# A fused attention, mixture-of-experts and MLP kernel: three kinds of instruction change places in the front end

## The chip, the cores and the metric

The kernel runs on one core of one Trainium2 chip. A core has five engines with queues of their own: TensorE (PE in the profile; its weight loads are PEld), VectorE (DVE), ScalarE (ACT), GpSimd (POOL) and SyncE (SP), which here issues most of the DMAs. Each engine takes its instructions in the order in which the program put them, so an instruction that waits holds up all that stand behind it on that engine. The metric is the device time of one execution in microseconds; lower is better.

## The reference

Three stages follow one another; the result of each is the input of the next. Only the last one's result is returned.

```python
def _attn_ref(q, k, v, phi):          # (4, 8, 576, 64), 32 memory slots
    a = np.exp(phi - np.max(phi, axis=2, keepdims=True))
    a = a / (np.sum(a, axis=2, keepdims=True) + 1e-09)
    k_m = np.einsum('bhsm,bhsd->bhmd', a, k)
    v_m = np.einsum('bhsm,bhsd->bhmd', a, v)
    scores = np.matmul(q, k_m.transpose(0, 1, 3, 2)) / np.sqrt(64)
    attn = softmax(scores)
    return np.matmul(attn, v_m)
def _moe_ref(x, w_gate, w_noise, noise, w1, w2):   # 2304 tokens, 512 wide, 8 experts of 1024
    noisy = x @ w_gate + np.log1p(np.exp(x @ w_noise)) * noise
    top2, top2_w = the two largest of noisy, softmax over these two
    for e in range(8):
        for k in range(2):
            mask = top2[:, k] == e
            out[mask] += top2_w[mask, k, None] * (np.maximum(x[mask] @ w1[e], 0.0) @ w2[e])
def _moe2_ref(x, w_in, w_out):        # 512 -> 2048 -> 512
    h = x @ w_in
    return (h * np.cos(h)) @ w_out
```

## The kernel before

**Stages.** The 2304 tokens are 18 tiles of 128, t0 to t17. The *front end* is the attention with the routing: four batches' memory keys and values (`k_gen(b)`), then the 18 tiles (`t_gen(t)`), then two routings, of tiles 0 to 7 (`route(0)`) and of tiles 8 to 17 (`route(1)`). The *experts* follow: each has a first product (`l1`, eight column groups f, 24 matmuls each for expert 0's first part) and a second (`l2`), run on tokens that POOL gathers by index (`xg`) and SP transposes (`x`). The MLP (`m1`, `m2_`) is last. Expert weights come as float32 (`raw`) and are split into a high and a low float16 half (`w`): four squares per weight for the scale (`junk`, line 176), four copies for the high halves (`w_hi`, line 201, on ACT), four subtractions for the low ones (`w_lo`, line 204, on DVE). The squares and splits of expert 0's weights lie between the attention's tiles on ACT.

**One batch, `k_gen`.** DVE takes the maximum of phi (`mx`, line 556), ACT the exponential (`ew`, 563), PE transposes it (`et`), ACT copies it out (`e`), PE makes keys and values (`kp`, 40 matmuls), DVE and ACT scale them (`kd`, 590; `vm`, 593), PE transposes the keys (`pk`), and DVE and ACT each copy a half of them into `bdk` (601, 602), which all tiles of the batch need. `bdv` holds the values.

**One tile, `t_gen`.** PE makes the scores (`sc`, 655), DVE subtracts their maxima (`smx`, 660; `sd`, 663), ACT takes the exponential, DVE the sum and its reciprocal (`ssm`, 668 and 669), POOL multiplies (`d`), PE transposes (`pt`), ACT copies (`e2T`, 677), PE makes the output (`x`, 685). ACT then reads `x` twice: the scaled rows (`xs`, 690) and the routing logits (`lgb`, line 696, shown as `rlgb` or `rt`). ACT makes the high float16 half (`hl`, 700), POOL the low one (701), and SP stores both. `x` has one buffer: the next tile's output waits until the logits are copied. The scores' buffers are halves of one tile, and so are those of `pt`.

**What sets the order.** Every step has a planned time (`at`, `stages`); `issue` writes the steps out by these times, and a scheduler then orders each engine's instructions by priority and by its own idea of when their inputs are there. `gated(key)` puts an instruction behind another, named one (`last[key]`), in that order; `chain` does so for a whole series. For expert 0's weights a table names what each square and split stands behind:

```python
(w_square, 0): ("t7A", "t8A", "t9A", "t10A"),
(w_hi, 0): ("t12A", "t13A", "t14A", "t15A"),
```

Here `t12A` is set by tile 12's copy `xs`. PE's `l1` for f = 2 stands behind the second routing's `rank` matmuls (`gated("rank")`, line 850), and these stand behind both f = 0 and f = 1 in PE's order.

Of the kernel before, what the change touches and what calls it, by code (L numbers as in the profile page):

```python
# [60 lines left out]
def fused_kernel(ctx, tc, phiT, qT, kv, wgn, noise, w1, w2, wi, wo, out):  # L61
# [154 lines left out]
    def chain(key, fn, *a, **kw):  # L216

        with gated(key):
            last[key] = fn(*a, **kw)  # L219
# [122 lines left out]
    def route(g):  # L342
# [25 lines left out]
        for k in range(2):  # L368
# [10 lines left out]
            if k == 0:  # L379
                V.scalar_tensor_tensor(y, oh[0][:, ts, :], -3.0e38, y, op0=OP.mult, op1=OP.add)  # L380
                yield
        V.tensor_tensor(m16[:, ts, :], oh[0][:, ts, :], oh[1][:, ts, :], op=OP.add)
        d = rg(g, "d", n)
# [164 lines left out]
    for k in range(2):  # L548
        bdk.append(ap.tile([P, 4, 2 * M], F32, tag=f"bdk{k}", name="bdk", bufs=1))
        G.memset(bdk[k], 0.0)  # L550

    def k_gen(b):

        ph = ph_t.pop(b)
        mx = ap.tile([P, 2], F32, tag="mx", name="mx", bufs=1)
        V.tensor_reduce(mx, ph, axis=AX.X, op=OP.max)
        V.tensor_scalar(mx, mx, -1.0, None, op0=OP.mult)
# [4 lines left out]
        for g in range(2):  # L562
            A.activation(ew[:, g, o:o + S], ph[:, g, :], AF.Exp, bias=mx[:, g:g + 1], accum_out=den[:, g:g + 1])
        V.tensor_scalar(den, den, eps, None, op0=OP.add)
# [24 lines left out]
        for g in range(2):  # L589
            V.tensor_scalar(kd[:, g], kp[:, g, None, 0:D].to_broadcast([P, 2, D]), den[:, g:g + 1], None, op0=OP.mult)  # L590
        vm = ap.tile([P, 2, D], F32, tag="vm", name="vm", bufs=1)
# [9 lines left out]
        last[f"bdk{b}V"] = V.tensor_copy(bk[0:64, :, 0:M], pv[0:64, :, 0, :])  # L601
        A.activation(bk[64:128, :, M:], pv[64:128, :, 1, :], AF.Copy)
        yield
# [45 lines left out]
    def t_gen(t):  # L649
# [39 lines left out]
        with gated(f"t{ahead}E"):  # L689
            last[f"t{t}A"] = A.activation(xs.rearrange("p (g d) -> p g d", g=2), x[:, :, 0:256], AF.Copy,  # L690
                                          scale=sT[:, 0, t:t + 1])
        g = ROUTE_OF[t]
        if t == GROUPS[g][0]:
            n = GROUPS[g][1] - GROUPS[g][0]
            lgb[g] = rg(g, "lgb", n, 2, 2 * E)
        A.activation(lgb[g][:, t - GROUPS[g][0]], x[:, :, 256:272], AF.Copy)
        yield
# [54 lines left out]
    for b in range(B):  # L752
        stages(k_gen(b), [k_start[b] + x for x in k_steps])
    for i in range(NT):
# [100 lines left out]
    def l1_out(e, part, f):  # L855
        n = (parts[part][1] - parts[part][0]) * P
        hi, lo = hT[e, part]
        ph = prod.pop((e, part, f))
        chain("A", A.activation, hi[:, f, :], ph[:, :n], AF.Relu)
        chain("V", V.scalar_tensor_tensor, lo[:, f, :], ph[:, :n], 0.0, hi[:, f, :], op0=OP.max, op1=OP.subtract)  # L860

# [406 lines left out]
```

## Time and profile before

| | us |
|---|---|
| three timed runs | 933.47, 937.98, 939.71 |
| their median | 937.98 |
| span of the profiled execution | 936.9 |
| PE busy in it | 883.3 (94%) |
| DVE, ACT, POOL busy | 581.2, 468.1, 213.1 |

The span runs from the first instruction to the last; the page gives no other time for the profiled execution, and it lies 1.1 us below the median and inside the spread of the three runs (6.2 us, 0.7%). PE is busy nearly all the time from the experts on, and not in the first seventh of the span. Busy shares of PE say little in themselves, since the ends of matmuls are modelled; the granted clock stands beside them.

### The profile page before, as it was taken

The page shows a single profiled execution, that of the slowest core. Times are in us where ns is not written, and L with a number is a line of the kernel's source. Part 1 is how long each engine was busy: PE and PEld are TensorE (multiplying, and loading weights), DVE is VectorE, ACT ScalarE, POOL GpSimd, SP SyncE. Part 2 cuts the span into 40 slices and gives each one's busy share as a digit, 9 for nine tenths or more (in the row PEclk, how much of TensorE's full clock was granted, in tenths as well). Part 3 has the DMA queues.
Part 4 walks back from the last instruction along what each step waited for, and adds up shares of the span by engine and source line. Part 5 has one row for each costly group of instructions (what it writes and reads, how often), then busy time and mean ns, then how long its engine had stood idle before and what let it go on. Part 6 is the DMA issues. An engine that isn't in the chain of part 4 may idle for free. (4 is left out here: it accounts for less than half of the span.)

```text
span 936.9 us, 14173 instructions
## 1 busy us (share of the span) xinstructions
PE 883.3 (94%) x5368; PEld 512.9 (55%) x5368; DVE 581.2 (62%) x1266; ACT 468.1 (50%) x830; POOL 213.1 (23%) x234
## 2 busy tenths in 40 slices
PE   4897489999999999999999999999999999999997
PEld 3676265655647475655646565564444444444564
DVE  2557572476757575776762457787875774555564
ACT  3487624666766676667772333444432432322242
POOL 1255312120010101010000124334432522221221
PEclk9897589999999999999999999999999999999999
DMA  9971239888797769799653454222401510200010
GB/s 350 396 270 68 91 83 268 268 220 296 243 303 240 206 242 292 250 263 336 206 185 136 114 202 90 69 68 57 102 1 12 130 40 1 78 12 1 1 45 23
DMA packets 108246, 146.55 MB, mean 156 GB/s; under 512 B 65808, under 2 KB 66448, under 8 KB 106128
## 3 DMA queue, kind: packets, MB, share of 16 engines
q1 hardware_dynamic: 89536, 103.56, 35.9%
q0 software_dynamic: 6080, 19.93, 7.4%
q10 hardware_dynamic: 12560, 22.13, 6.7%
q8 instruction: 43, 0.70, 0.3%
q14 instruction: 27, 0.22, 0.1%
HBM read 95.26 MB, written 35.13 MB: 139 GB/s over the span
## 5 line engine op out<-in xcount | busy, mean ns | idle before, releaser
L219 PE MATMUL h<-x,w 128*128 128x384 f16 (+1 forms) x1536 | 215.3, 301 | 9.7 <-DMA x<-xg 9.3
L219 PE MATMUL y<-w,hT 128*128 128x512 f16 x960 | 210.7, 379 | 2.2 <-issue 2.2
L219 PE MATMUL g<-x2T,win 128*128 128x256 f16 (+1 forms) x1152 | 202.5, 326 | 5.8 <-DVE ty L1043 4.4
L219 PE MATMUL o<-wout,gT 128*128 128x512 f16 x864 | 202.1, 379 | 0.2
L219 PEld LDWEIGHTS <-w 128*128 128x128 f16 x1536 | 151.5, 99 | 68.7 <-DMA x<-xg 8.8
L219 PEld LDWEIGHTS <-win 128*128 128x128 f16 x1152 | 112.6, 98 | 90.2 <-issue 8.0
L219 PEld LDWEIGHTS <-hT 128*128 128x128 f16 x960 | 93.8, 99 | 111.4 <-issue 2.7
L1045 POOL TENSOR_TENSOR gT<-ty,gT 128x256 f16<-128x256 f32 (+1 forms) x96 | 92.7, 967 | 252.8 <-ACT gT L1044 252.7
L1042 ACT ACTIVATE tt<-tt,hp 128x256 f32<-128x256 f32 (+1 forms) x96 | 58.9, 614 | 164.3 <-DVE tt L1041 150.1
L219 PEld LDWEIGHTS <-gT 128*128 128x128 f16 x864 | 84.1, 98 | 93.4 <-POOL gT L1045 2.1
L219 DVE SCALAR_TENSOR_TENSOR w<-raw,wsc,w 128x1024 f16<-128x1024 f32 x64 | 81.1, 1288 | 32.6 <-ACT w L219 32.6
L219 DVE SCALAR_TENSOR_TENSOR hT<-h,hT 128x384 f16<-128x384 f32 (+1 forms) x128 | 61.4, 487 | 63.2 <-ACT hT L219 62.9
L1039 DVE SCALAR_TENSOR_TENSOR ty<-g,wis,bct 128x256 f32<-128x256 f32 (+1 forms) x96 | 58.8, 612 | 65.1 <-PE g L219 65.1
L219 ACT ACTIVATE hT<-h 128x384 f16<-128x384 f32 (+1 forms) x128 | 55.3, 435 | 73.4 <-PE h L219 70.5
L1043 DVE SCALAR_TENSOR_TENSOR ty<-g,fac,tt 128x256 f32<-128x256 f32 (+1 forms) x96 | 59.1, 616 | 52.8 <-ACT tt L1042 52.2
L1044 ACT ACTIVATE gT<-ty 128x256 f16<-128x256 f32 (+1 forms) x96 | 50.2, 523 | 64.5 <-DVE ty L1043 64.4
L219 ACT ACTIVATE w<-raw,wsc 128x1024 f16<-128x1024 f32 x64 | 71.6, 1139 | 4.4 <-ACT o L219 2.1
L825 POOL DMA_INDIRECT xg<-xd,idxB x24 | 24.1, 1006 | 218.3 <-DMA x<-xg 207.7
L1041 DVE SCALAR_TENSOR_TENSOR tt<-tt,ty 128x256 f32<-128x256 f32 (+1 forms) x96 | 68.9, 718 | 2.6
L219 ACT ACTIVATE junk<-raw 128x1024 bf16<-128x1024 f32 x64 | 67.3, 1051 | 3.9 <-ACT o L219 3.4
L219 ACT ACTIVATE o<-y,ysc 128x512 f32<-128x512 f32 x40 | 27.4, 686 | 70.6 <-PE y L219 70.4
L963 POOL DMA_INDIRECT y<-yd,sidx x36 | 36.3, 1010 | 88.4 <-DMA yd<-o 80.7
(234 smaller groups left out, 714.1 us busy)
## 6 DMA issues: line engine op xcount, KB each, us to landing
raw<-in_w SPq DMA_DIRECT2D x32, 1024.0 KB, 9.1
yd<-o ACTq DMA_DIRECT2D x40, 256.0 KB, 5.0
kvt<-in_kv SPq DMA_DIRECT2D x9, 1024.0 KB, 15.6
cvt<-in_wi SPq DMA_DIRECT2D x8, 1024.0 KB, 6.5
wst<-cvt SPq DMA_DIRECT2D x16, 512.0 KB, 3.4
cvt<-in_wo SPq DMA_DIRECT2D x8, 1024.0 KB, 9.1
yd<-zero ACTq DMA_DIRECT2D x13, 512.0 KB, 5.5
xd<-hl SPq DMA_DIRECT2D x18, 256.0 KB, 2.1
```

The costliest lines, as they stand in the source:

```text
L219: last[key] = fn(*a, **kw)
L825: G.indirect_dma_start(out=g, out_offset=None, in_=xd[0:NA * P] if part == 0 else xd, in_offset=bass.IndirectOffsetOnAxis(ap=idx[:, col:co ...
L963: G.indirect_dma_start(out=y, out_offset=None, in_=yd[0:rows], in_offset=bass.IndirectOffsetOnAxis(ap=sidx[:, t, k:k + 1], axis=0))
L1039: V.scalar_tensor_tensor(y, ph[:, :n], wis[:, 2 * E + c:2 * E + c + 1], bct[j], op0=OP.mult, op1=OP.mult)
L1041: V.scalar_tensor_tensor(t, t, MAGIC, y, op0=OP.subtract, op1=OP.subtract)
L1042: A.activation(t, t, AF.Sin, bias=hp, scale=-2.0 * math.pi)
L1043: V.scalar_tensor_tensor(y, ph[:, :n], fac[:, c:c + 1], t, op0=OP.mult, op1=OP.mult)
L1044: A.activation(g[:, 0, :n], y, AF.Copy)
L1045: G.tensor_tensor(g[:, 1, :n], y, g[:, 0, :n], op=OP.subtract)
```

## The change

Five edits, all in the order of the front end; no instruction's work changes.

1. `last["t{t}A"]` is set by the copy of the logits in place of the copy `xs`. What the table puts behind a tile (a square or a split of expert 0's weights) now stands behind the logits.
2. The maxima of phi of batches 1, 2 and 3 are put behind other work on DVE: behind batch 0's scaled keys, behind tile 0's reciprocal, behind tile 3's.
3. Batch 1's exponentials are put behind ACT's half of batch 0's `bdk`, and batch 1's first step is planned at 16.9 in place of 15.0.
4. The first low half of `hT` (expert 0, part 0, f = 0) is put behind the second routing's mask sum `m16`.
5. Two keys are set for this (`kd0`, `bdk0A`, `m16` with the routing's number).

```diff
-        V.tensor_tensor(m16[:, ts, :], oh[0][:, ts, :], oh[1][:, ts, :], op=OP.add)
+        last[f"m16{g}"] = V.tensor_tensor(m16[:, ts, :], oh[0][:, ts, :], oh[1][:, ts, :], op=OP.add)
...
+    MX_AFTER = {1: "kd0", 2: "t0V", 3: "t3V"}
...
-        V.tensor_reduce(mx, ph, axis=AX.X, op=OP.max)
+        with gated(MX_AFTER.get(b)):
+            V.tensor_reduce(mx, ph, axis=AX.X, op=OP.max)
...
-            A.activation(ew[:, g, o:o + S], ph[:, g, :], AF.Exp, bias=mx[:, g:g + 1], accum_out=den[:, g:g + 1])
+            with gated("bdk0A" if b == 1 else None):
+                A.activation(ew[:, g, o:o + S], ph[:, g, :], AF.Exp, bias=mx[:, g:g + 1], accum_out=den[:, g:g + 1])
...
-            last[f"t{t}A"] = A.activation(xs.rearrange("p (g d) -> p g d", g=2), x[:, :, 0:256], AF.Copy,
+            A.activation(xs.rearrange("p (g d) -> p g d", g=2), x[:, :, 0:256], AF.Copy,
                                           scale=sT[:, 0, t:t + 1])
...
-        A.activation(lgb[g][:, t - GROUPS[g][0]], x[:, :, 256:272], AF.Copy)
+        last[f"t{t}A"] = A.activation(lgb[g][:, t - GROUPS[g][0]], x[:, :, 256:272], AF.Copy)
...
-        stages(k_gen(b), [k_start[b] + x for x in k_steps])
+        stages(k_gen(b), [16.9 if b == 1 and x == -8.0 else k_start[b] + x for x in k_steps])
...
-        chain("V", V.scalar_tensor_tensor, lo[:, f, :], ph[:, :n], 0.0, hi[:, f, :], op0=OP.max, op1=OP.subtract)
+        with gated("m161") if (e, part, f) == (0, 0, 0) else nullcontext():
+            chain("V", V.scalar_tensor_tensor, lo[:, f, :], ph[:, :n], 0.0, hi[:, f, :], op0=OP.max, op1=OP.subtract)
```

Line numbers of the changed kernel are 3 to 5 higher from the edits on (690 becomes 694, 655 becomes 659).

**ACT at tile 13**, before and then changed: `xs_1131` is tile 13's copy, `rt_887` the logits of the second routing, `w_1101` the high half of expert 0's first weight.

```order
L690 ACTIVATE xs_1131<-x_1117,sT_108 128x512
L219 ACTIVATE w_1101<-raw_634,wsc_113 128x1024
L696 ACTIVATE rt_887<-x_1117 128x32
L677 ACTIVATE e2T_1144<-pt_155 128x256
L700 ACTIVATE hl_1135<-xs_1131 128x512
```

```order
L694 ACTIVATE xs_1131<-x_1117,sT_108 128x512
L700 ACTIVATE rt_887<-x_1117 128x32
L219 ACTIVATE w_1101<-raw_634,wsc_113 128x1024
L681 ACTIVATE e2T_1144<-pt_155 128x256
L704 ACTIVATE hl_1135<-xs_1131 128x512
```

The split and the logits have changed places; it is so at tiles 12 to 15 with the splits and at tiles 7 to 10 with the squares.

**PE at tiles 11 to 13**, before and then changed: `x_1035`, `x_1069` and `x_1117` are the outputs of tiles 11, 12 and 13, the two `sc` rows the scores of tiles 16 and 17, `sums` belongs to the weights' scale.

```order
L655 MATMUL sc_154<-bdk_141,qt_632 128x64 x4
L685 MATMUL x_1035<-bdv_712,e2T_955 128x272 x2
L219 MATMUL sums_1022<-wmx_109,ones32_111 128x5
L675 MATMUL pt_155<-ident_73,d_1045 128x128 x2
L655 MATMUL sc_154<-bdk_141,qt_632 128x64 x4
L685 MATMUL x_1069<-bdv_712,e2T_1032 128x272 x2
L675 MATMUL pt_155<-ident_73,d_1079 128x128 x2
```

```order
L689 MATMUL x_1035<-bdv_712,e2T_955 128x272 x2
L659 MATMUL sc_154<-bdk_141,qt_632 128x64 x4
L219 MATMUL sums_1022<-wmx_109,ones32_111 128x5
L679 MATMUL pt_155<-ident_73,d_1045 128x128 x2
L689 MATMUL x_1069<-bdv_712,e2T_1032 128x272 x2
L679 MATMUL pt_155<-ident_73,d_1079 128x128 x2
L659 MATMUL sc_154<-bdk_141,qt_632 128x64 x4
```

The outputs of tiles 11 and 12 now stand ahead of the scores of tiles 16 and 17.

**DVE from the end of batch 0 on**, before and then changed: `mx_263` and `mx_274` are batch 1's maximum, `mx_422` batch 2's, `kd_273` and `kd_263` batch 0's keys, `smx_337` and `smx_391` the maxima of tiles 0 and 1, `ssm_386` tile 0's sum.

```order
L556 TENSOR_REDUCE mx_263<-ph_161 128x2
L557 TENSOR_SCALAR mx_263<-mx_263 128x2
L590 TENSOR_SCALAR kd_273<-kp_222,den_198 128x128 x2
L601 COPY bdk_139<-pk_279 64x4x32
L564 TENSOR_SCALAR den_268<-den_268 128x2
L565 RECIPROCAL den_268<-den_268 128x2
L660 TENSOR_REDUCE smx_337<-sc_154 128x8
L560 MEMSET ew_425 128x2x64
L663 TENSOR_TENSOR sd0_143<-sc_154,smx_337 128x8x32
L668 TENSOR_REDUCE ssm_386<-sd0_143 128x8
L556 TENSOR_REDUCE mx_422<-ph_161 128x2
L669 RECIPROCAL ssm_386<-ssm_386 128x8
```

```order
L594 TENSOR_SCALAR kd_263<-kp_222,den_198 128x128 x2
L559 TENSOR_REDUCE mx_274<-ph_161 128x2
L605 COPY bdk_139<-pk_269 64x4x32
L560 TENSOR_SCALAR mx_274<-mx_274 128x2
L568 TENSOR_SCALAR den_279<-den_279 128x2
L569 RECIPROCAL den_279<-den_279 128x2
L664 TENSOR_REDUCE smx_337<-sc_154 128x8
L667 TENSOR_TENSOR sd0_143<-sc_154,smx_337 128x8x32
L672 TENSOR_REDUCE ssm_386<-sd0_143 128x8
L673 RECIPROCAL ssm_386<-ssm_386 128x8
L559 TENSOR_REDUCE mx_422<-ph_161 128x2
L664 TENSOR_REDUCE smx_391<-sc_154 128x8
```

Batch 1's maximum has moved behind batch 0's keys, and batch 2's behind the whole of tile 0's row work; batch 3's, further on, from ahead of tile 2's `smx` to behind tile 3's reciprocal.

## Rows read from the trace of the kernel before

**Rows 1.** Stretches of the span: length, engines' busy time, granted clock, DMA share.

```profile
core 0 of [0], span 936.9 us
core 0: us, PE busy (x) PEld busy (x) DVE busy (x) ACT busy (x) POOL busy (x), PEclk, DMA share, GB/s
40.00:50.00 10.00, 10.00 (x102) 7.33 (x102) 4.28 (x15) 5.39 (x15) 4.38 (x5) 0.86 1.04 389
80.00:90.00 10.00, 8.47 (x32) 5.89 (x32) 7.91 (x35) 4.88 (x13) 3.69 (x5) 0.52 0.14 53
160.00:200.00 40.00, 40.00 (x257) 24.96 (x256) 25.21 (x59) 26.62 (x44) 7.27 (x8) 1.00 0.83 251
```

**Rows 2.** Timeline, tiles 12 to 17: start, us, engine, line, operation [idle before, releaser].

```profile
85.93 0.69 ACT L690 ACTIVATE xs<-x,sT 128x512 f32<-128x512 f32 x1 [2.39 <-PE x L685]
86.52 1.14 ACT L219 ACTIVATE w<-raw,wsc 128x1024 f16<-128x1024 f32 x1
...
87.55 0.19 ACT L696 ACTIVATE rt<-x 128x32 f32<-128x32 f32 x1
87.63 0.38 ACT L677 ACTIVATE e2T<-pt 128x256 f32<-128x256 f32 x1
...
87.79 2.09 PE L685 MATMUL x<-bdv,e2T 128*64 128x272 f32 x8 [1.53 <-ACT rt L696]
...
88.20 0.64 ACT L700 ACTIVATE hl<-xs 128x512 f16<-128x512 f32 x1
...
90.00 0.69 ACT L690 ACTIVATE xs<-x,sT 128x512 f32<-128x512 f32 x1 [1.06 <-PE x L685]
...
102.42 0.69 ACT L690 ACTIVATE xs<-x,sT 128x512 f32<-128x512 f32 x1 [1.54 <-PE x L685]
...
103.24 2.18 PE L685 MATMUL x<-bdv,e2T 128*128 128x272 f32 x4 [0.93 <-ACT rt L696]
...
105.52 0.69 ACT L690 ACTIVATE xs<-x,sT 128x512 f32<-128x512 f32 x1 [0.78 <-PE tab L433]
```

**Rows 3.** Timeline, tiles 10 and 11 with the scores of tile 16.

```profile
76.45 0.69 ACT L690 ACTIVATE xs<-x,sT 128x512 f32<-128x512 f32 x1
...
78.98 1.10 PE L655 MATMUL sc<-bdk,qt 128*128 128x64 f32 x8 [1.17 <-DVE sbt L629]
...
79.92 1.64 PE L685 MATMUL x<-bdv,e2T 128*128 128x272 f32 x4
...
81.66 0.69 ACT L690 ACTIVATE xs<-x,sT 128x512 f32<-128x512 f32 x1 [2.16 <-PE x L685]
```

**Rows 4.** Timeline, maxima of phi of batches 1 to 3 and their neighbours.

```profile
14.90 1.35 DVE L556 TENSOR_REDUCE mx<-ph 128x2 f32<-128x1152 f32 x1 [4.01 <-DMA ph<-in_phiT]
...
16.36 0.60 DVE L590 TENSOR_SCALAR kd<-kp,den 128x128 f32<-128x128 f32 x2
...
25.79 1.35 DVE L556 TENSOR_REDUCE mx<-ph 128x2 f32<-128x1152 f32 x1 [1.03 <-DMA ph<-in_phiT]
...
28.05 0.61 DVE L590 TENSOR_SCALAR kd<-kp,den 128x128 f32<-128x128 f32 x2
...
35.16 1.35 DVE L556 TENSOR_REDUCE mx<-ph 128x2 f32<-128x1152 f32 x1 [2.64 <-DMA ph<-in_phiT]
36.43 0.41 DVE L660 TENSOR_REDUCE smx<-sc 128x8 f32<-128x256 f32 x1
...
37.35 1.10 PE L655 MATMUL sc<-bdk,qt 128*128 128x64 f32 x8 [2.59 <-DVE sd L663]
```

**Rows 5.** Timeline, from the last tile to the experts.

```profile
107.98 1.16 POOL L701 TENSOR_TENSOR hl<-xs,hl 128x512 f16<-128x512 f32 x1 [1.95 <-issue]
...
119.44 5.30 PE L219 MATMUL h<-x,w 128*128 128x256 f16 x24 [8.71 <-DMA x<-xg]
...
122.63 0.42 DVE L219 SCALAR_TENSOR_TENSOR hT<-h,hT 128x256 f16<-128x256 f32 x1 [3.89 <-ACT hT L219]
...
124.53 0.33 PE L390 MATMUL rank<-m,after 128*128 128x80 f16 x1
...
145.32 11.86 PE L219 MATMUL h<-x,w 128*128 128x384 f16 x72 [0.60 <-DMA x<-xg]
```

More of the change, by code (lines that the diff above doesn't have):

```diff
@@ L589, in k_gen @@
         for g in range(2):
-            V.tensor_scalar(kd[:, g], kp[:, g, None, 0:D].to_broadcast([P, 2, D]), den[:, g:g + 1], None, op0=OP.mult)
+            last[f"kd{b}"] = V.tensor_scalar(kd[:, g], kp[:, g, None, 0:D].to_broadcast([P, 2, D]), den[:, g:g + 1], None, op0=OP.mult)
         vm = ap.tile([P, 2, D], F32, tag="vm", name="vm", bufs=1)
@@ L601, in k_gen @@
         last[f"bdk{b}V"] = V.tensor_copy(bk[0:64, :, 0:M], pv[0:64, :, 0, :])
-        A.activation(bk[64:128, :, M:], pv[64:128, :, 1, :], AF.Copy)
+        last[f"bdk{b}A"] = A.activation(bk[64:128, :, M:], pv[64:128, :, 1, :], AF.Copy)
         yield
```

## The prediction, made before the changed kernel ran

> **What bounds the kernel now.** The stretches first. From 160 us on PE is busy for 40.00 of 40.00 us at full clock [rows 1], and PE waits only 0.60 us, for gathered tokens, when the experts' main part begins at 145.32 [rows 5]. What follows runs as one PE queue with its work in a fixed order, so an edit of the front end is worth what it moves the start at 145.32, and no more. The reader should look for stretches ahead of that point where PE does not set the pace: 80 to 90 us, where its granted clock is 0.52, so the lower of the two levels (1.2 of 2.4 GHz) almost throughout [rows 1]. Read backwards, 145.32 hangs on the first `l1` at 119.44, which waited 8.71 us for gathered tokens. POOL issues these gathers right behind the last tile's low half (107.98 + 1.16 = 109.14), and that hangs on tile 17's `xs` at 105.52 [rows 2, 5]. So the time of tile 17's `xs` is the quantity to forecast; the 119.44 - 105.52 = 13.9 us behind it have the same instructions in the same order before and after.
>
> **Part one: the splits behind the logits.** Tiles 12 to 17 form a ring through ACT and PE: `xs` reads `x`, then the logits are read, then PE may write the next `x`. In the ring of tile 12 the split starts 0.59 us after `xs` and the logits only 1.03 us after the split; PE's next `x` then starts at 87.79, having waited 1.53 us for just these logits [rows 2]. The same pattern stands four times (tiles 12 to 15), from 85.93 to 102.42: 16.49 / 4 = 4.12 us each. Tile 16's ring has no split ahead of the logits: 105.52 - 102.42 = 3.10 us, of which 0.82 us go by from `xs` to the next `x` and 2.18 us are that `x` [rows 2]. With the split behind the logits all five should take 3.10. Does the split then stand in the way of something else? It runs beside the 2.18 us of the matmuls: split 1.14, `e2T` 0.38 and `hl` 0.64 make 2.16 us [rows 2], which is just covered; without that cover each further tenth on ACT would show in the ring. Gain: 4 x 1.02 = 4.1, less 0.2 because the first routing's three `rank` matmuls (0.33 us for one, [rows 5]) now stand between two of these outputs: **3.9 us**. Bounds: nothing, if the 4.12 were set elsewhere; at most ACT's own work in a ring, 0.59 + 1.03 + 0.08 us by starts and 0.38 + 0.64 behind them = 2.72 us, so (4.12 - 2.72) x 4 + 0.4 for the fifth = 6.0 us.
>
> The squares at tiles 7 to 10 change places in the same way. ACT was the full engine there, so I count nothing for the places themselves, but their new order lets tiles 11 and 12 go earlier, which is the next term.
>
> **Part two: outputs ahead of scores at tiles 11 and 12.** In the old order the scores of tile 16 stand ahead of tile 11's output, and they waited until 78.98 for DVE; the output came at 79.92, and `xs` at 81.66 had waited 2.16 us for it [rows 3]. Tile 12's `xs` waited 2.39 us in the same way, behind the scores of tile 17 [rows 2]. Now both outputs stand ahead of those scores, which nobody needs so soon: tiles 16 and 17 come to their own turn four rings later. At most both waits go, 4.5 us; at least nothing, if the low clock makes PE as late as before. ACT also has work of its own in these two rings (exponentials, `hl`, the square of tile 10, now behind the logits), so I take a little over half, **2.5 us**.
>
> **Part three: the maxima of phi.** This part has a good and a bad side. Good: DVE waited for batch 3's phi until 35.16, 2.64 us, then spent 1.35 us on its maximum, and only then came tile 2's `smx`; PE idled 2.59 us until 37.35 in consequence [rows 4]. Now that maximum stands behind tile 3, when phi has long landed. Also batch 0's keys, which stood behind batch 1's maximum (14.90 + 1.35, keys at 16.36), can start as soon as PE is done, over 1 us earlier, and tile 0's scores no longer stand behind batch 1's transposes. Bad: batch 2's phi landed at 25.79, and tile 0's row work will now be done before that, so DVE will stand idle some 4 us in front of batch 2's maximum, with tile 1's `smx` queued behind it. And the rows between that maximum and batch 1's keys grow from seven tiny ones to eleven or so, four of them of about 0.4 us (`smx` 0.41, [rows 4]), one waiting for ACT. I put these keys at about 30.1 instead of 28.05, and everything of batch 2 follows them: `vm`, its exponentials, its transposes, its `kp`.
>
> Which side wins? From 40 to 50 us PE is busy 10.00 of 10 [rows 1]: once that stage begins the remaining work of the batches and tiles is a fixed queue on PE, and what counts is how much PE idles before. The change removes the 2.59 us and adds about 1.0 us in front of batch 1's later key transposes (30.1 + 0.6 for the keys, while PE has nothing else ready). Net **1.6 us** gained. Bounds: a gain of 2.64 + 1.35 = 4.0 us, if nothing new is late; a loss of 2.1 us, the lateness of batch 1's keys, if batch 2 becomes the chain that the tiles wait for.
>
> **Part four: the masks.** DVE waited 3.89 us, until 122.63, to make the first low half, with the last three mask steps queued behind it [rows 5]. Now these go first, so `m16` is ready about 4 us sooner. But PE runs 24 matmuls of f = 0 and 1 from 119.44 to 124.74 ahead of the `rank` matmuls, which ran at 124.53 [rows 5] at once: they did not wait for the masks. What is left is a DVE queue shorter by a few small rows up to the gathers of part 1, whose lateness cost PE 0.60 us at 145.32. I take **0.3 us**, between 0 and 0.6. The first low half loses nothing: ACT's high half comes later than the masks anyway.
>
> **The sum.** 3.9 + 2.5 + 1.6 + 0.3 = 8.3 us. The profiled span of 936.9 would become 928.6; against the median of 937.98, which lies 1.1 us above the span, this gives **929.7 us**.
>
> **Rivals.**
>
> *The front is full anyway (934).* Only part one and part four hold: the 1.6 us of the phi part are lost to batch 2's later keys, and tiles 11 and 12 stay as late as before since PE's outputs take twice as long at the low clock. 937.98 - 4.2 = 933.8. For it: the low clock in the rows [rows 1]; against it: the two waits of 2.16 and 2.39 us on rows whose order has changed [rows 2, 3].
>
> *The clock comes back (926).* In the old trace PE had its low clock in all of the late tiles. With rings of 3.10 us PE would be busy for 2.18 and another 0.6 for `pt`, nine tenths of the time. If the clock rose there, `x` would take half of 2.18 us and the ring would fall to ACT's 2.72 us: 6.0 for part one, 4.5 for part two, 1.6 and 0.3, 12.4 us in all, 925.6. Against it: from 80 to 90 us PE was busy 8.47 of 10 and stayed at the low level [rows 1]. The Trainium skill, in "TensorE: Matmul & The Clock Gate" (Part 1, The HAM clock gate), says that the throttled state is the default and sustained activity releases it; by that rule the denser rings could bring the full clock and this rival's 926, while the row of 80 to 90 us speaks for staying low and the forecast's 929.7. I give it a sixth.
>
> *Batch 2 becomes the late one (slower: 940).* Place: DVE in front of batch 2's maximum. Mechanism: tile 1's `smx` and batch 1's keys queue behind a DMA wait that ends at 25.79 [rows 4]. Price: keys 2.1 us late, then `vm`, two exponentials and copies that queue on ACT behind tiles which now come first; if each of the four steps slips by one tile copy (0.69 us for `xs`, [rows 2]) more, `kp` of batch 2 ends 2.1 + 2.8 = 4.9 us later. As PE then idles in the stage of 40 to 50 us, its clock may fall there too, 1.5 us more. It decides when the loss exceeds the 4.2 us of parts one and four while part two gives nothing: 937.98 + 6.4 - 4.2 = 940.2. Against it: tiles 2 and 3 now have work ready for PE in that stage. One in ten.
>
> *A part does not do what it says.* For the masks this is in the sum already: the wait that they are moved away from was not PE's.
>
> **How the numbers follow.** Forecast (927 to 933) 0.52; the full front (933 to 936) 0.2; clock back (under 927) 0.17; batch 2 late (over 937) 0.1; the rest 0.01. A measurement of this kernel can tell about 1%, 9.4 us, from no change: the three runs alone spread over 6.2 us. Faster by over 1% means under 928.6: all of the clock's 0.17 and a quarter of the forecast, 0.30. Slower by over 1%, over 947.4, needs more than the slow rival: 0.02. Within 1%: 0.68. For the range I cut most of the slow rival and the far end of the clock's: 924 to 936.5.
>
> **What would show it.** Right: `xs` of tiles 12 to 17 about 3.1 us apart with `x` starting 0.8 us after each; no wait of over 1 us on PE at tiles 11 and 12; DVE waiting some 4 us ahead of the second maximum and not at all ahead of the fourth; tile 17's `xs` at about 97.5; the first `l1` 13.9 us later, at about 111.4; the experts' main part at about 137. The masks ahead of the first low half, with `rank` still directly behind f = 1. Wrong: rings still near 4 us, or ACT never idle in them; granted clock above 0.5 there; PE idle for over 3 us between 28 and 45 us; or a distance from tile 17's `xs` to the first `l1` other than 13.9 us, which would mean that the gathers hang on something that I have not seen.

## The result, and the profile after

The changed kernel takes 927.19 us (median of 7 runs, 926.32 to 928.36), the kernel before 935.74 us (7 runs, 930.41 to 939.71). The ratio is 0.9905, with a 95% interval from 0.9877 to 0.9934: 0.9% faster, 8.55 us by the medians. The profiled execution after took 926.95 us with a span of 925.1, so 1.85 us lie around the span. With as much around it, the profiled execution of before (span 936.9) took 938.75 us, 3.0 above its median. The two traces therefore differ by 11.8 us, and 3 us of that are the execution of before that the profiler caught.

The stretches of the changed kernel answer to [rows 1] (length, busy time of the engines, granted clock, DMA share, GB/s):

```profile
core 0: us, PE busy (x) PEld busy (x) DVE busy (x) ACT busy (x) POOL busy (x), PEclk, DMA share, GB/s
30.00:40.00 10.00, 9.90 (x136) 8.59 (x136) 7.44 (x22) 8.61 (x26) 4.67 (x7) 1.00 1.03 398
40.00:50.00 10.00, 10.00 (x96) 7.77 (x92) 5.99 (x21) 7.80 (x22) 5.09 (x8) 1.00 1.04 392
70.00:80.00 10.00, 7.90 (x54) 5.88 (x53) 9.81 (x34) 8.33 (x21) 6.04 (x7) 1.00 0.20 79
80.00:90.00 10.00, 6.65 (x19) 4.07 (x19) 8.74 (x37) 8.06 (x18) 4.38 (x6) 0.56 0.22 82
```

From 30 to 50 us PE no longer stops and keeps its full clock; before, 40 to 50 us had a granted clock of 0.86. DVE, which had been busy for 7.84 of the 10 us from 70 to 80, is now full there (9.81). The clock still falls after 80 us.

Tiles 12 to 17 in the timeline (start, us, engine, line, operation, idle before and its releaser) answer to [rows 2]:

```profile
76.36 0.67 ACT L694 ACTIVATE xs<-x,sT 128x512 f32<-128x512 f32 x1
76.92 0.19 ACT L700 ACTIVATE rt<-x 128x32 f32<-128x32 f32 x1
77.00 1.15 ACT L219 ACTIVATE w<-raw,wsc 128x1024 f16<-128x1024 f32 x1
77.17 1.14 PE L689 MATMUL x<-bdv,e2T 128*64 128x272 f32 x8
...
79.59 0.67 ACT L694 ACTIVATE xs<-x,sT 128x512 f32<-128x512 f32 x1
...
80.40 1.36 PE L689 MATMUL x<-bdv,e2T 128*128 128x272 f32 x4 [1.42 <-ACT rt L700]
...
82.16 0.69 ACT L694 ACTIVATE xs<-x,sT 128x512 f32<-128x512 f32 x1
...
83.53 0.27 PE L390 MATMUL rank<-m,after 128*128 128x64 f16 x1 [1.77 <-DVE m L382]
...
84.19 2.02 PE L689 MATMUL x<-bdv,e2T 128*128 128x272 f32 x4
...
86.31 0.69 ACT L694 ACTIVATE xs<-x,sT 128x512 f32<-128x512 f32 x1 [0.97 <-PE x L689]
...
89.41 0.69 ACT L694 ACTIVATE xs<-x,sT 128x512 f32<-128x512 f32 x1 [0.51 <-PE x L689]
...
92.52 0.69 ACT L694 ACTIVATE xs<-x,sT 128x512 f32<-128x512 f32 x1 [0.78 <-PE tab L433]
```

The split (`w`, 77.00) now stands behind the logits (76.92), and the next output starts 0.81 us after `xs`, as forecast. The rings, however, are 3.23, 2.57, 4.15, 3.10 and 3.11 us: the outputs of tiles 13 and 14 run at full clock or nearly (1.14 and 1.36 us; tile 13's took 2.09 before), where ACT and the logits set the pace; in the third PE stops 1.77 us for the masks of the *first* routing (`rank`, 83.53), with tile 15's transposes behind it; only the last two are the rings of the forecast.

Tiles 10 and 11 answer to [rows 3], DVE's early rows to [rows 4]:

```profile
70.08 0.69 ACT L694 ACTIVATE xs<-x,sT 128x512 f32<-128x512 f32 x1
...
71.28 1.16 PE L689 MATMUL x<-bdv,e2T 128*128 128x272 f32 x4
...
73.00 0.70 ACT L694 ACTIVATE xs<-x,sT 128x512 f32<-128x512 f32 x1
```

```profile
16.13 0.61 DVE L594 TENSOR_SCALAR kd<-kp,den 128x128 f32<-128x128 f32 x2 [5.20 <-PE kp L589]
16.65 1.34 DVE L559 TENSOR_REDUCE mx<-ph 128x2 f32<-128x1152 f32 x1
...
25.54 1.35 DVE L559 TENSOR_REDUCE mx<-ph 128x2 f32<-128x1152 f32 x1 [3.07 <-DMA ph<-in_phiT]
...
30.00 0.61 DVE L594 TENSOR_SCALAR kd<-kp,den 128x128 f32<-128x128 f32 x2 [0.85 <-PE kp L589]
...
37.20 1.30 DVE L559 TENSOR_REDUCE mx<-ph 128x2 f32<-128x1152 f32 x1
```

Tile 11's `xs` no longer waits for PE (2.16 us before). DVE waits 3.07 us in front of batch 2's maximum and not at all in front of batch 3's, and batch 1's keys come at 30.00, where 30.1 was forecast.

From the last tile to the experts, to be read beside [rows 5]:

```profile
94.98 1.16 POOL L705 TENSOR_TENSOR hl<-xs,hl 128x512 f16<-128x512 f32 x1 [1.96 <-issue]
...
106.32 0.24 DVE L382 TENSOR_TENSOR m<-oh,oh 128x80 f16<-128x80 f32 x1
106.43 5.30 PE L219 MATMUL h<-x,w 128*128 128x256 f16 x24 [8.71 <-DMA x<-xg]
...
109.63 0.42 DVE L219 SCALAR_TENSOR_TENSOR hT<-h,hT 128x256 f16<-128x256 f32 x1 [3.07 <-ACT hT L219]
...
111.53 0.33 PE L390 MATMUL rank<-m,after 128*128 128x80 f16 x1
```

The main part in PE's rows:

```profile
132.54 11.86 PE L219 MATMUL h<-x,w 128*128 128x384 f16 x72 [0.49 <-DMA x<-xg]
```

The masks (`m`, 106.32) are done 0.13 us after the first `l1` starts (before, they started at 123.51, 4.07 us behind it), and still `rank` stands 5.10 us behind that `l1` (5.09 before).

Where the 11.8 us of the two traces lie, by stretches between the same rows (`xs` of a tile, first `l1`, main part, end):

| stretch | before | after | difference |
|---|---|---|---|
| start to tile 6 | 63.37 | 56.35 | -7.02 |
| tile 6 to 10 | 13.08 | 13.73 | +0.65 |
| tile 10 to 12 | 9.48 | 6.28 | -3.20 |
| tile 12 to 17 | 19.59 | 16.16 | -3.43 |
| tile 17 to first `l1` | 13.92 | 13.91 | -0.01 |
| first `l1` to main part | 25.88 | 26.11 | +0.23 |
| main part to the end | 791.58 | 792.56 | +0.98 |

### The profile page after: what moved, and what is told of

Same layout as the page of the kernel before. It is cut to its first block, busy times and chain, and to the rows that moved or that the text cites. A ratio compares the mean times of both kernels' runs of the same rounds, so it can differ in the third digit from the quotient of the medians.

```text
span 925.1 us, 14179 instructions
## 1 busy us (share of the span) xinstructions
PE 879.5 (95%) x5368; PEld 511.0 (55%) x5368; DVE 582.4 (63%) x1266; ACT 467.7 (51%) x830; POOL 215.4 (23%) x234
```

## The experiments

Theory: the gain comes from three independent places, and these add up: the front (batch 3's maximum out of the way), tiles 11 and 12, and the rings of tiles 12 to 17; the masks give nothing. The main rival: the late tiles set the pace by themselves, so that what the front gains is taken back. All ratios are against runs of the kernel before on the same chip. This table holds what the text below reads; its times are starts in each kernel's trace, in us.

| kernel | `xs` of tile 6 | tile 12 | tile 17 | first `l1` | main part | median | ratio, interval |
|---|---|---|---|---|---|---|---|
| before | 63.37 | 85.93 | 105.52 | 119.44 | 145.32 | 935.74 | 1 |
| changed | 56.35 | 76.36 | 92.52 | 106.43 | 132.54 | 927.19 | 0.9905, 0.9877 to 0.9934 |
| splits alone | 61.34 | 79.97 | 94.70 | 108.53 | 134.36 | 928.03 | 0.991, 0.9877 to 0.9944 |
| phi alone | 56.34 | 79.70 | 99.29 | 113.25 | 139.37 | 932.88 | 0.9958, 0.9934 to 0.9981 |
| masks alone | 62.66 | 85.32 | 104.92 | 118.57 | 144.75 | 937.86 | 1.0011, 0.9983 to 1.0039 |
| no gate on batch 2 | 56.32 | 76.33 | 92.50 | 106.34 | 131.57 | 926.97 | 0.9904, 0.9872 to 0.9937 |
| batch 3's gate alone | 56.36 | 81.46 | 101.05 | 115.07 | 140.02 | 931.15 | 0.9959, 0.994 to 0.9978 |
| splits, masks, batch 3's gate | 58.67 | 78.48 | 95.25 | 108.94 | 135.00 | 926.78 | 0.9911, 0.9881 to 0.994 |
| squares late | 56.93 | 76.94 | 93.10 | 106.55 | 132.47 | 926.48 | 0.9911, 0.9887 to 0.9936 |
| rank late | 56.64 | 76.64 | 91.78 | 105.60 | 130.69 | 924.92 | 0.9892, 0.9866 to 0.9918 |
| 20 fillers | 56.79 | 76.80 | 92.97 | 108.15 | 131.57 | 925.53 | 0.9899, 0.9874 to 0.9925 |
| rank late, 12 fillers | 57.04 | 77.05 | 91.30 | 106.62 | 130.31 | 923.82 | 0.988, 0.985 to 0.9911 |
| rank late, ring fillers | 56.37 | 76.37 | 88.86 | 105.39 | 131.29 | 926.21 | 0.9905, 0.9876 to 0.9934 |
| rank late, both fillers | 57.00 | 77.01 | 89.50 | 106.00 | 132.46 | 925.9 | 0.9863, 0.9836 to 0.989 |

**Splits alone.** The kernel before with edit 1:

```diff
-            last[f"t{t}A"] = A.activation(xs.rearrange("p (g d) -> p g d", g=2), x[:, :, 0:256], AF.Copy,
+            A.activation(xs.rearrange("p (g d) -> p g d", g=2), x[:, :, 0:256], AF.Copy,
...
-        A.activation(lgb[g][:, t - GROUPS[g][0]], x[:, :, 256:272], AF.Copy)
+        last[f"t{t}A"] = A.activation(lgb[g][:, t - GROUPS[g][0]], x[:, :, 256:272], AF.Copy)
```

> The kernel before with edit 1 alone (splits and squares behind the logits). Theory (the gains of the front and of the late tiles add up): tiles 12 to 17 come 3.1 to 3.5 us apart in place of 4.1, tiles 11 and 12 some 2 to 3 us earlier, tile 6 where it was; 4 to 6.5 us faster than before, so a ratio of about 0.994. Rival (the late tiles set the pace by themselves, whatever the front does): this edit alone gives nearly all, 8 us, ratio 0.991. Second rival (the low clock of the late tiles hides it): under 2 us, ratio 0.998 or more.

Measured: 7.6 us faster than the runs beside it (935.61), which is the rival's number. Tile 12 to 17 take 14.73 us (19.59 before, 16.16 in the changed kernel), tile 10 to 12 take 6.05. So terms one and two are both this edit's, and alone it does more in the late tiles than in company. A second reading was not expected: this kernel has the front of before, instruction by instruction up to tile 6, and yet reaches tile 6 at 61.34, 2.0 us earlier. Its stretches tell why:

```profile
20.00:30.00 10.00, 10.00 (x118) 8.11 (x117) 4.16 (x14) 2.27 (x6) 0.62 (x1) 0.50 1.04 401
30.00:35.00 5.00, 5.00 (x26) 4.91 (x26) 2.44 (x8) 3.47 (x12) 1.80 (x3) 0.50 1.04 390
35.00:40.00 5.00, 5.00 (x67) 4.03 (x67) 3.33 (x9) 3.84 (x12) 1.50 (x2) 1.00 1.03 408
40.00:50.00 10.00, 9.91 (x116) 7.63 (x114) 5.77 (x21) 7.07 (x22) 3.78 (x5) 1.00 1.04 389
```

In this execution PE had the low clock from 20 to 35 us, so it was still busy when batch 3's phi landed, did not stop, and kept the full clock afterwards. In the trace of before it had the full clock at 30 us, ran dry (1.94 of 5 us busy from 35 to 40) and had the low clock again at 40. The same instructions in the same order thus differ by 2 us from one execution to another. A third execution of that front, in the masks alone, ran dry as well (PE busy for 2.55 of 5 us from 35 to 40) and reached tile 6 at 62.66.

**Phi alone.** Edits 2 and 3 without the splits and the masks (their code as in the diff above).

> The kernel before with the edits of phi alone (maxima of batches 1 to 3 behind other rows, batch 1's exponentials behind the keys' copy). Theory: PE's wait near 35 us and the cold stretch at 39 to 42 us go, tile 6 comes about 6 us earlier than before, and this is kept to the end: 4 to 6 us faster, ratio about 0.995. Rival (lost later): tile 6 comes 6 us earlier, but tiles 11 to 17, with the splits still ahead of the logits, take it back; under 2 us, ratio 0.998 or more. The forecast's own value was 1.6 us, ratio 0.998, with tile 6 1.6 us earlier.

Measured: tile 6 at 56.34 as in the changed kernel, and the 6.2 us against before are still there at tile 17 (99.29). By the medians only 2.7 us are left, partly because the execution of before in the trace is a late one. Tile 10 to 12 take 9.48 us, to the hundredth what they took before, and tiles 12 to 17 19.59: nothing of terms one and two comes from phi. By the medians the two gains come to 7.6 + 2.7 = 10.3, and both together give 8.6; the difference of 1.7 us is within the intervals (some 3 us to either side for the splits, 2 for phi). That they do not add up is seen in the traces, one execution each: at tile 17 phi is worth 6.2 us alone, and 2.2 us with the splits in place (94.70 against 92.52).

**Masks alone.** The kernel before with edit 4:

```diff
-        chain("V", V.scalar_tensor_tensor, lo[:, f, :], ph[:, :n], 0.0, hi[:, f, :], op0=OP.max, op1=OP.subtract)
+        with gated("m161") if (e, part, f) == (0, 0, 0) else nullcontext():
+            chain("V", V.scalar_tensor_tensor, lo[:, f, :], ph[:, :n], 0.0, hi[:, f, :], op0=OP.max, op1=OP.subtract)
```

> The kernel before with edit 4 alone (first low half behind the masks). Theory: nothing beyond 0.3 us; rank still starts 5.1 us after the first l1, and the main part 25.9 to 26.1 us after it; ratio 0.999 to 1.001. Rival (masks carry part of the gain): main part 0.6 us or more nearer to the first l1. Its front is that of before, so its profile also shows how far the front of before differs from one execution to the next.

Measured: no difference (the interval holds 1); `rank` 5.10 us and the main part 26.18 us behind the first `l1`.

**No gate on batch 2.** The changed kernel with

```diff
-    MX_AFTER = {1: "kd0", 2: "t0V", 3: "t3V"}
+    MX_AFTER = {1: "kd0", 3: "t3V"}
```

> The changed kernel without the gate on batch 2's maximum, which then goes back to where the scheduler puts it. Theory (batch 1's keys at 30.0 us in place of 28 cost nothing, since PE has batch 1's other work and tile 0's output to do): within 1 us of the changed kernel, ratio to before about 0.991, PE busy over 9.5 of 10 us between 30 and 40. Rival (the wait of 3 us in front of batch 2's maximum costs something): 1 to 3 us faster than the changed kernel, ratio 0.988 to 0.990. Second rival (the gate is what brings tile 0's and tile 1's rows early and so the gain): 2 us or more slower than the changed kernel, ratio 0.993 or more.

Measured: every `xs` up to tile 17 within 0.4 us of the changed kernel, and the same time. But this run tests neither the theory nor the rivals: without the gate the scheduler writes the same order, on all four engines and to the end, and DVE waits in front of batch 2's maximum as it did:

```profile
25.18 1.35 DVE L559 TENSOR_REDUCE mx<-ph 128x2 f32<-128x1152 f32 x1 [2.94 <-DMA ph<-in_phiT]
```

So it amounts to six more runs of the changed kernel (926.53 to 927.15), and its main part at 131.57 in place of 132.54 shows how far two executions of one order lie apart there. That the later keys of batch 1 cost nothing at tile 6 is seen in other traces: the keys start at 30.00 in the changed kernel, at 28.80 in phi alone and at 27.87 with batch 3's gate alone (next), and tile 6 comes at 56.35, 56.34 and 56.36.

**Batch 3's gate alone**, on the kernel before:

```diff
+    MX_AFTER = {3: "t3V"}
...
-        V.tensor_reduce(mx, ph, axis=AX.X, op=OP.max)
+        with gated(MX_AFTER.get(b)):
+            V.tensor_reduce(mx, ph, axis=AX.X, op=OP.max)
```

> The kernel before with one edit of phi alone: batch 3's maximum behind tile 3's reciprocal; batches 1 and 2 as before. Theory (the stop of PE near 35 us behind that maximum is the costly one, and the low clock at 40 us follows from it): PE's wait of 2.6 us there is gone, tile 6 comes 3 us or more earlier than before, and some 2 us are left at the end, as with the whole phi part (2.7 us by the medians). Rival (what counts is batch 1's maximum behind batch 0's keys): the wait near 35 us goes but tile 6 moves by under 1 us, and the time is that of before.

The stretches of this kernel:

```profile
30.00:40.00 10.00, 9.92 (x126) 7.80 (x126) 6.38 (x21) 7.51 (x24) 4.33 (x6) 1.00 1.04 398
40.00:50.00 10.00, 9.79 (x99) 7.71 (x94) 5.71 (x19) 7.56 (x23) 4.67 (x6) 1.00 1.04 391
```

Tile 6 (56.36) is within 0.02 us of all the phi edits together, PE neither stops nor loses its clock from 30 to 50 us, and 4.2 us are left at the end. So by the time this one gate gives all of part three (4.2 us against 2.7 of the phi edits together, with overlapping intervals). Behind tile 6 its trace is the later one: batch 3's keys at 60.51 against 58.86 in phi alone, tile 17 at 101.05 against 99.29.

**Splits, masks and batch 3's gate**, the changed kernel with one gate of phi left:

```diff
-    MX_AFTER = {1: "kd0", 2: "t0V", 3: "t3V"}
+    MX_AFTER = {3: "t3V"}
...
-            with gated("bdk0A" if b == 1 else None):
+            with nullcontext():
...
-        stages(k_gen(b), [16.9 if b == 1 and x == -8.0 else k_start[b] + x for x in k_steps])
+        stages(k_gen(b), [k_start[b] + x for x in k_steps])
```

> The changed kernel with one gate of phi left, that of batch 3's maximum (batches 1 and 2 planned and ordered as before; splits and masks as changed). Theory (batch 3's gate carries the front's gain, the other two and batch 1's later exponentials carry nothing): tile 6 at 56.4 us or earlier, time within 1 us of the changed kernel's 927.2. Rival (the other gates matter once the splits are out of the way): 1.5 us or more slower, 928.7 or above.

Measured: the time of the changed kernel, but tile 6 at 58.67, not at 56.4 or earlier. In the profiled execution the granted clock was 0.71 from 30 to 40 us. The gates on batches 1 and 2 and batch 1's later exponentials are not needed for the time. They may guard against such executions: nine traces have the front with all of them (phi alone, the changed kernel and seven made from it), and tile 6 lies between 56.32 and 57.04 in all nine, though the granted clock from 20 to 30 us was 0.50 in some (rank late, 56.64) and 1.00 in others (12 fillers, 57.04). With batch 3's gate alone there are two traces, 56.36 and 58.67.

**Squares late.** The changed kernel with the squares of expert 0's second weight behind tile 17's high half:

```diff
-        A.activation(hv[:, 0], xs, AF.Copy)
+        last[f"t{t}H"] = A.activation(hv[:, 0], xs, AF.Copy)
...
-        (w_square, 1): ("t16A", "t17A", "t17A", "t17A"),
+        (w_square, 1): ("t17H", "t17H", "t17H", "t17H"),
...
-        at(a_of(17) + 8.0 + 0.01 * c, e0, w_square, 1, c)
+        at(a_of(17) + 8.5 + 0.01 * c, e0, w_square, 1, c)
```

> The changed kernel with the four squares of expert 0's second weight behind tile 17's high half in place of behind tiles 16 and 17's logits. Theory (the first l1 hangs on tile 17's xs through its high half and POOL's low half): POOL's low half starts 1.4 us behind xs in place of 2.46, the first l1 12.9 us behind it in place of 13.9, and 0.8 to 1 us less in the end. Rival (the gathers or the experts' weights are later than that by themselves): distance still 13.9 us, or the main part no nearer, time as that of the changed kernel, 927.2.

Measured: POOL's low half starts 1.49 us behind `xs` but takes 1.78 us in place of 1.16, the distance to the first `l1` is 13.45, and the main part is not nearer (132.47): `rank` now waits 0.87 us for the second routing's masks. The time is 0.7 us below the changed kernel's with overlapping ranges: inconclusive, and nearer to the rival.

**Rank late.** The changed kernel with `rank` of the first routing behind tile 15's output:

```diff
-    for t, n in ((12, 7), (13, 7), (14, 6)):
+    for t, n in ((12, 7), (13, 7), (14, 2)):
...
+    at(a_of(17) + 2.3, advance, r0, 4, "t15P")
```

> The changed kernel with the first routing's rank behind tile 15's output in PE's order (in the changed kernel PE stands still for 1.77 us in front of rank, with tile 15's transposes behind it, and the granted clock falls just there). Theory A (that stop is what brings the low clock in): tile 15's xs 0.5 to 1.5 us earlier, tiles 16 and 17 2.6 us apart in place of 3.1 at full clock, tile 17's xs 2 us or more earlier, 2 us less in the end. Theory B (the clock falls by itself there, since PE's share of work has been thin for several tiles): tile 15 0.5 us earlier, tiles 16 and 17 still 3.1 us apart, under 1 us in the end.

PE's rows at tile 15:

```profile
83.29 2.18 PE L689 MATMUL x<-bdv,e2T 128*128 128x272 f32 x4 [0.62 <-ACT rt L700]
85.26 0.30 PE L390 MATMUL rank<-m,after 128*128 128x64 f16 x1
```

`rank` no longer waits and tiles 14 to 17 take 9.32 us in place of 10.36, so the stop had cost 1.04 us. But tile 15's output has the low clock without the stop too (2.18 us at 83.29): theory B on the clock. At the end 2.3 us are gained by the medians (922.21 to 926.51 against 926.32 to 928.36), which is theory A's time; the main part starts 1.85 us earlier.

**20 fillers in front of the first `l1`** (matmuls whose product is not used), in the changed kernel:

```diff
+    def fill(n):
+        fb = trk("fill")
+        for _ in range(n):
+            with gated(f"t{NT - 1}P"):
+                T.matmul(fb, lhsT=after, rhs=wt[0][:, 0, 0:512], start=True, stop=True)
+
+    at(tA + 0.0019, fill, 20, lead=LA)
```

> The changed kernel with 20 more matmuls of 128x512 (float16, product not used) on PE behind the sums, in its wait of 8.7 us in front of the first l1; nothing else is computed from them. Theory (the low clock at 106 to 112 us is a cost of its own): the fillers take 4 to 8.5 us, the granted clock rises in them or soon after, the first l1 takes 2.7 to 4 us in place of 5.3, the main part starts 2 to 3 us earlier and the time falls by 1 to 2.5 us. Rival (the masks, the half splits and the gathers of part 1 set the main part's start, PE's speed there doesn't matter): first l1 short, but main part within 0.5 us of 132.5 and no gain. On the bad side: the fillers end after the gathers have landed and delay the first l1.

PE's rows in front of the experts:

```profile
101.49 6.83 PE L1088 MATMUL fill<-w,after 128*128 128x512 f16 x20 [3.31 <-DVE wnm L219]
108.15 2.78 PE L219 MATMUL h<-x,w 128*128 128x256 f16 x24
```

The first `l1` takes 2.78 us in place of 5.30, but starts at 108.15, since the fillers end late; 1.7 us are gained by the medians, while the main part (131.57) is no earlier than in that repeat of the changed kernel. Both the gain and the bad side came.

**Rank late and 12 fillers.**

> The changed kernel with rank behind tile 15's output and 12 matmuls of 128x512 (product not used) in PE's wait in front of the first l1. With 20 of them the last one ended 1.2 us after the gathers had landed, and about 12 of their 6.8 us went by at the low clock. Theory (both costs are separate): the fillers end by the time the gathers land, the first l1 starts at about 105.7 us and takes 2.7 to 3.5 us, the main part at 129 to 130 us; 922.5 to 924 us, 1 to 2.5 us less than with rank alone (924.9). Rival (behind the first l1 other work sets the pace: the gathers of part 1, and the MLP's start gives the rest back): main part at 130 us or later, time within 0.7 us of 924.9.

Measured: the first `l1` at 106.62 for 2.79 us, the main part at 130.31 and 923.82 us, 1.1 us below rank alone, with overlapping ranges. The time is the theory's, the main part the rival's; the first `l1` came 0.9 us later than expected, since the fillers ended at 106.32 and the gathers landed another 0.3 us later (below). All six runs (921.19 to 925.48) lie under all seven of the changed kernel: the version with the lowest median of all, 0.988 of before.

**Rank late and ring fillers.** Behind each output of tiles 12 to 17:

```diff
+    def ring_fill(t):
+        fb = trk("fill")
+        for _ in range(12):
+            with gated(f"t{t}P"):
+                T.matmul(fb[:, 0:P], lhsT=after, rhs=iota_r, start=True, stop=True)
+
+    for t in range(12, NT):
+        at(a_of(t) + 7.21, ring_fill, t)
```

> The changed kernel with rank behind tile 15's output and, behind the output of each of tiles 12 to 17, 12 matmuls of 128x128 on PE whose product is not used. It asks what the fall of the clock at 82 us costs and whether PE's idle time brings it. Theory A (PE's gaps bring the low clock): granted clock 1.00 to 92 us, tiles 14 to 17 2.6 us apart (ACT's own work) in place of 3.1, tile 17's xs at about 90.3 in place of 91.8, 1.5 us less. Theory B (not the gaps): the clock falls as before, the fillers take 1.3 us of each ring at the low clock, of which some 0.9 us is free, so rings of 3.3 us or more and a time of 925 to 927 us.

The stretch of 80 to 90 us with rank alone and then with the ring fillers, the index on DVE and the first gather on POOL:

```profile
80.00:90.00 10.00, 7.29 (x20) 4.37 (x21) 8.32 (x32) 8.99 (x19) 4.78 (x6) 0.61 0.22 85
```

```profile
80.00:90.00 10.00, 7.98 (x71) 6.10 (x70) 9.28 (x33) 10.00 (x23) 5.27 (x6) 1.00 0.27 106
```

```profile
94.84 0.17 DVE L438 TENSOR_SCALAR idxA<-tab 128x16 int32<-128x16 f32 x1 [0.23 <-PE tab L433]
```

```profile
95.31 2.01 POOL L838 DMA_INDIRECT xg<-xd,idxA  x1 [2.74 <-DVE tabB L439]
```

The clock and the rings are theory A's, the time (926.21) is theory B's. The clock stays at 1.00 through tile 17, the rings fall to 2.47, 2.46 and 2.21 us with ACT busy for 10.00 of 10 us, and tile 17's `xs` (88.86) is 2.9 us earlier than with rank alone. Nothing of it reaches the experts: the first `l1` comes 16.5 us behind `xs` in place of 13.9, because POOL, done with the low half, now waits 2.74 us for the index (`idxA`, `tabB`) that DVE makes from the first routing's table.

**Both fillers**, 18 of them in front of the first `l1` and behind the sums.

> The changed kernel with rank behind tile 15's output, the 12 small matmuls behind each of tiles 12 to 17, and 18 matmuls of 128x512 behind the sums in front of the first l1 (products not used): PE at full clock from tile 12 to the experts, as far as fillers can do that. Theory (with the clock up, DVE's table of the first routing sets the gathers and its masks of the second set rank): tile 17's xs at 88.9, the first l1 still at 105.4, rank waiting for the masks until 109.3 to 110, main part at 130 to 131, time 923 to 925: no better than the 923.8 with fillers in one place. Rival (each fall of the clock costs what its rows show, and the gains add up): first l1 at 104.5 or earlier, main part at 128.5, 921 to 922.

The theory's direction: 925.9 us, no better than 12 fillers in one place; the first `l1` at 106.00, `rank` at 110.28, the main part at 132.46, later than either expected. But `rank` did not wait for the masks (done at 106.28), as the theory had it: the fillers ended 2.2 us before the gathers landed, and the first `l1` took 4.44 us, so part of it had the low clock again. Its ratio (0.9863) is the lowest, since the kernel before took 938.18 us beside it and 935.01 beside the 12 fillers; its median is 2.1 us above theirs, with overlapping ranges. Which of the two kernels is faster is not decided.

## Why the prediction was right, and where its steps were not

**The total.** 8.3 us were forecast and 8.55 measured, 929.7 against 927.19 since the forecast started from a median of three runs 2.2 us above that of seven. But the terms are 3.9 + 2.5 + 1.6 + 0.3, and the traces show 3.4 + 3.2 + 7.0 - 0.2, less 0.65 and 0.98 given back on the way. The sum came out right with one term far too small, because later stretches took back a part and because the trace of before was of a late execution; that these made up for each other is luck. In the quantity that the prediction named there was no such help: tile 17's `xs` was put at about 97.5 and came at 92.52, 13.0 us earlier than before in place of 8.0, and the main part, put at about 137, at 132.54.

**Part three is the mis-sized step.** I priced PE's idle time of 2.59 us and took 1.0 off for batch 1's keys. Tile 6 came 7.0 us earlier (5.0 against the splits alone, which have the front of before), beyond the bound of 4.0. The keys came where I put them (30.00), and cost nothing at tile 6. By the time the gain is batch 3's gate alone. For its size, the stretches of before:

```profile
30.00:35.00 5.00, 4.50 (x44) 3.57 (x44) 1.09 (x5) 3.18 (x11) 0.97 (x2) 1.00 1.03 392
35.00:40.00 5.00, 1.94 (x33) 1.58 (x34) 3.62 (x9) 2.47 (x8) 0.90 (x2) 0.94 1.03 409
```

They give 0.50 + 3.06 us of idle PE between 30 and 40 us (4.50 and 1.94 of 5 busy), of which the changed kernel keeps 0.10; and a granted clock of 0.94 and 0.86 from 35 to 40 and 40 to 50 us, which at two levels is 0.6 and 2.8 us at the low one, half of it lost, 1.7. That makes 5.2, an estimate from busy times that are modelled. The rest of the 7.0, some 1.9, is order and not speed. Tile 6's output now stands ahead of 54 of batch 3's 80 `kp`, before it stood ahead of 14; these rows follow that output, in the changed kernel and then in that of before:

```profile
56.13 0.64 PE L589 MATMUL kp<-kvt,e 128*32 128x128 f32 x16
...
57.52 1.29 PE L589 MATMUL kp<-kvt,e 128*32 128x128 f32 x38
```

```profile
63.26 0.64 PE L585 MATMUL kp<-kvt,e 128*32 128x128 f32 x14
```

Batch 3's keys need all 80 in both kernels, and they come 5.08 us earlier:

```profile
63.95 0.61 DVE L590 TENSOR_SCALAR kd<-kp,den 128x128 f32<-128x128 f32 x2 [0.66 <-PE kp L585]
```

```profile
58.87 0.61 DVE L594 TENSOR_SCALAR kd<-kp,den 128x128 f32<-128x128 f32 x2 [0.34 <-PE kp L589]
```

The row with 0.86 stood in [rows 1]: I read it for PE's busy 10.00 and not for its clock, as though what an idle stretch costs ended with it.

**What became of it.** The bound on what counts was also drawn wrongly: "once that stage begins the remaining work of the batches and tiles is a fixed queue on PE". With the splits in place, 5.0 us of earliness at tile 6 (61.34 against 56.35) are 2.2 at tile 17, 1.8 at the main part and 0.8 in the medians. From 60 to 70 us ACT is busy for 9.93 of 10, from 70 to 80 DVE for 9.81; and PE meets `rank` before its masks are done, which cost 1.04 us.

```profile
60.00:70.00 10.00, 8.21 (x79) 6.76 (x79) 6.33 (x18) 9.93 (x29) 5.48 (x8) 1.00 0.52 184
```

How much each of these took back is shown for `rank` alone. So the first rival (*the front is full anyway*) was right that a part of the gain is lost behind phi, but not in how: it named batch 2's later keys, which came at 44.34 in place of 47.79, and late outputs at tiles 11 and 12, which came earlier.

**Part one** gave 3.4 where 3.9 was forecast, but as rings of 2.57 to 4.15 us, not of 3.10. The logits free PE 0.8 us after `xs`, as forecast; the 0.2 us for `rank` was in truth a stop of 1.77 us, since the masks stand on DVE behind tiles that now come sooner; and two rings ran at full clock or nearly. **Part two** gave 3.2 where 2.5 was forecast; it is all edit 1's. **Part four** gave nothing, for the reason stated: `rank` did not wait for the masks.

**The clock's rival** came about in part: the granted clock was 1.00 up to 80 us and 0.56 from 80 to 90, so the low level began near 81 us, at tile 14's output in place of tile 11's, though PE was busy for only 7.90 of 10 us before that, less than the nine tenths to which I had tied it. By the prediction's own list a granted clock above 0.5 in these rings was a sign of being wrong, and in the first of them it stood at 1.00. The ring fillers show that the full clock can be kept there, and that the gain of 12.4 us which I had put on it does not follow: they took 926.21 us, 8.8 less than the kernel before beside them and no less than rank alone, since the table of the first routing takes over. The prediction quoted the Trainium skill, "TensorE: Matmul & The Clock Gate" (Part 1, The HAM clock gate), that activity releases the throttle; the granted 1.00 with ring fillers beside 0.61 without them (80 to 90 us) agrees; in time no gain is seen.

**The distances.** Tile 17's `xs` to the first `l1` was 13.91 us, as fixed as forecast, as long as POOL's low half comes last; with the ring fillers it was 16.5. What stays the same is its distance from the first gather, 10.1 us in both (gathers at 96.31 and 95.31). And the main part, 12.78 us earlier, left 11.8 at the end: PE waits 3.13 us for the MLP's first inputs (`ty`) at 566.01 us, before 1.88 us at 577.32, and the 12 matmuls behind that wait take 2.72 us in place of 1.47 (granted clock 0.58 from 566 to 570, before 1.00 from 577 to 581). That too runs against "one PE queue with its work in a fixed order" from 145.32 on. What these inputs hang on was not tried.

## What to carry to other kernels

Price an idle stretch of TensorE with the granted clock of the rows behind it, not with its length alone: here the one was 3.5 us and the other, by the estimate above, 1.7. Measure an earlier start at a point that needs the same work in both kernels, as batch 3's keys do (5.1 us) and tile 6's copy does not (7.0). When several edits each free an engine in turn, do not add up their gains (at tile 17 phi was worth 6.2 us alone and 2.2 behind the splits): ask of each stage which engine is full next, and whether a wait behind it that was covered before, here for a routing's masks, now ends last. Profile a kernel whose runs spread by 1% more than once, since the row that an edit is aimed at may be one execution's. And see that an experiment's edit has changed the order before reading its time: the gate on batch 2 had not.

## What was not expected of the hardware

The same front has its low clock at different places in different executions (0.50 from 20 to 35 us, or 0.71 from 20 to 30 and 0.86 from 40 to 50), with 2 us between them at tile 6. With all edits of phi the low clock lay in different places as well, and tile 6 within 0.7 us. The kernel before spread over 10.2 us in 23 runs on one chip (929.33 to 939.54), the changed one over 2.0 in seven, the splits alone over 2.4 in six, phi alone over 5.5 in twelve, rank late over 4.3 in six. That the places of the front's low clock make up this spread is not shown, since one execution of each was profiled; and the splits alone, which keep the front of before, speak against it.

DVE's rows of the table take about 1.0 us longer when POOL's low half runs beside them. With rank late and 12 fillers, the same four `ohp` take

```profile
93.42 1.70 DVE L431 TENSOR_SCALAR ohp<-iota_r,pf 128x128 f16<-128x128 f16 x4
93.76 1.15 POOL L705 TENSOR_TENSOR hl<-xs,hl 128x512 f16<-128x512 f32 x1 [1.03 <-issue]
```

while with rank alone, where POOL's row starts after them, they take

```profile
93.01 0.73 DVE L431 TENSOR_SCALAR ohp<-iota_r,pf 128x128 f16<-128x128 f16 x4
...
94.24 1.16 POOL L705 TENSOR_TENSOR hl<-xs,hl 128x512 f16<-128x512 f32 x1 [1.92 <-issue]
```

An earlier tile 17 brings POOL's low half into the table, which delays the index, which delays the gathers: with rank late and 12 fillers the index is made at 95.97 in place of 94.59 and the first gather starts at 96.44 in place of 95.57, and that is why the first `l1` came late there. The Trainium skill, "SBUF — State Buffer" (Who interferes with whom), has it that DVE in a mode that uses two ports, which `tensor_scalar` can enter, contends with GpSimd for a shared pair of ports, and that whichever starts first holds the pair for its whole instruction while the other blocks. The 0.97 us between 1.70 and 0.73, beside a row of 1.15 us, agrees; which mode these rows ran in no run here shows.
